# Weight remainders and the rescaling of high words moved to GpSimd in a fused attention, MLP and expert kernel

## The chip, the cores and the metric

The kernel runs on one core of a Trainium2 chip. The metric is the device time of one execution in microseconds; the time before is the median of three runs. TensorE (PE) does matmuls, VectorE (DVE) and ScalarE (ACT) elementwise work, GpSimd (POOL) elementwise work and the issue of indirect DMAs, SyncE (SP) issues the other DMAs. Each engine runs its own queue in order and waits on semaphores for the others.

## The reference

Three layers on 4608 tokens of width 512:

```python
# 1. attention over keys and values that are means of 8 neighbours (576 -> 72), 8 batches, 8 heads of 64
scores = q @ k_pooled.T / 8;  attn = softmax(scores);  x = attn @ v_pooled
# 2. MLP with softplus, 512 -> 2048 -> 512
h = x @ w_in;  g = maximum(h, 0) + log1p(exp(-abs(h)));  x = g @ w_out
# 3. tokens with x @ w_skip > 0 go to the best of 8 experts (512 -> 1024 -> 512), gated
out[do] = xc + gate * (relu(xc @ w1[e]) @ w2[e]);  the other rows of out are x
```

The MLP's weights w_in and w_out reach the kernel as 64-bit floats, read as pairs of 32-bit words ("wbits"); the kernel makes 32-bit floats of them itself.

## The kernel before

**Precision by pairs.** Each matmul operand is kept as a rounded part and a remainder (xh and xl, wh and wl, gh and gl), and a product is three matmuls: high by high, high by low, low by high. The remainder is the value less its rounded part, one subtraction with two inputs in SBUF.

**Stages.** The first layer and the MLP run together, in 9 groups of 512 tokens. `p1(g, c)` computes chunk c (of 16) of the hidden layer for group g (12 matmuls into a bank h, L700), then the softplus: three ScalarE steps (L703 to L705), VectorE's L706 (reads h from PSUM and a from SBUF), ScalarE's rounding L708 and VectorE's remainder L710. `p2` multiplies the result with the output weights (12 matmuls, L721 to L723), two chunks behind p1. The attention for group g + 1 is fed in between as four units of small steps; its softmax shares are multiplied on GpSimd (L536), and its scores are turned with SyncE's "et" transfers (L644). After the groups come the experts, which this change does not touch.

**The weights.** They stay in SBUF for all groups and are unpacked once, during the attention of group 0 and the MLP of group 0, by `load_weights`, a generator that the main loop advances step by step. For each chunk a DMA brings the raw words; `unpack` rescales the high words by a power of two (L467) and turns the low words into small integers (L469), both on ScalarE; `join` puts them together with two VectorE operations (L472, L474), each with two SBUF inputs; ScalarE rounds (L489 or L511); VectorE subtracts (L491 or L512). Chunks 0 to 3 go in halves of 512 columns (L491), chunks 4 to 15 as two halves of 1024 for each pair of chunks' tile: the raw words stand in a tile raw and the result takes the same place as a tile wt. Within one such pair the loop reads:

```python
for j in range(2):
    lo, hi = raw[:, j, :, 0], raw[:, j, :, 1]
    unpack(lo, hi)
    yield
    v = scratch.tile([P, 1024], I32, tag="raw", name="v")
    join(v, lo, hi)
```

**What sets the order.** A scheduler places the instructions of the first two layers on each engine's queue when the kernel is built, by the program's order and its own estimate of when inputs are ready; so a changed engine moves other instructions too. The experts' part is in hand-written order.

Of the kernel before, what the change touches and what calls it, by code (L numbers as in the profile page):

```python
# [9 lines left out]
F32 = mybir.dt.float32  # L10
# [4 lines left out]
AF = mybir.ActivationFunctionType  # L15
ALU = mybir.AluOpType
# [18 lines left out]
def tile_kernel(ctx, tc, qT, kT, vT, wbits, w9, w1, w2, out):  # L35
    nc = tc.nc
# [379 lines left out]
    def wtile(slot, name, *shape, dtype=F32):  # L416
        return wpool.tile([P, *shape], dtype, tag=f"w{slot}", name=name)

    with ExitStack() as ph:
# [41 lines left out]
        def load_weights():  # L461


            bits = wbits.bitcast(I32)

            def unpack(lo, hi):
                nc.scalar.activation(out=hi.bitcast(F32), in_=hi.bitcast(F32), func=AF.Copy,  # L467
                                     scale=2.0 ** -112)
                nc.scalar.activation(out=lo, in_=lo.bitcast(U32), func=AF.Copy, scale=7.49 * 2.0 ** -32)  # L469

            def join(v, lo, hi):
                nc.vector.scalar_tensor_tensor(out=v, in0=hi, scalar=3, in1=lo,  # L472
                                               op0=ALU.logical_shift_left, op1=ALU.bitwise_or)
                nc.vector.scalar_tensor_tensor(out=v, in0=hi, scalar=-0x80000000, in1=v,  # L474
                                               op0=ALU.bitwise_and, op1=ALU.bitwise_or)

            for c in range(EARLY):
                if c % 2 == 0:
                    wt.append(wtile(c // 2, f"wt{c // 2}", 2, 2, 1024, dtype=F32R))
                for j in range(2):  # L480
                    wh, wl = (wt[c // 2][:, c % 2, i, j * 512:(j + 1) * 512] for i in range(2))
                    raw = scratch.tile([P, 512, 2], I32, tag="raw", name="raw")
                    nc.sync.dma_start(out=raw.rearrange("p a b -> p (a b)"),
                                      in_=bits[c * P:(c + 1) * P, j * 1024:(j + 1) * 1024])
                    lo, hi = raw[:, :, 0], raw[:, :, 1]
                    unpack(lo, hi)
                    yield
                    join(lo, lo, hi)
                    nc.scalar.activation(out=wh, in_=lo.bitcast(F32), func=AF.Copy)  # L489
                    yield  # L490
                    nc.vector.tensor_tensor(out=wl, in0=lo.bitcast(F32), in1=wh.bitcast(F32),  # L491
                                            op=ALU.subtract)
                    yield
            for i in range(EARLY // 2, 8):
                raw = wtile(i, f"raw{i}", 2, 1024, 2, dtype=I32)
                for j in range(2):
                    c = 2 * i + j
                    nc.sync.dma_start(out=raw[:, j].rearrange("p a b -> p (a b)"), in_=bits[c * P:(c + 1) * P, :])
                vs = []
                for j in range(2):  # L500
                    lo, hi = raw[:, j, :, 0], raw[:, j, :, 1]
                    unpack(lo, hi)
                    yield
                    v = scratch.tile([P, 1024], I32, tag="raw", name="v")
                    join(v, lo, hi)
                    vs.append(v.bitcast(F32))
                    yield
                wt.append(wtile(i, f"wt{i}", 2, 2, 1024, dtype=F32R))
                for j in range(2):
                    wh, wl = wt[i][:, j, 0], wt[i][:, j, 1]  # L510
                    nc.scalar.activation(out=wh, in_=vs[j], func=AF.Copy)  # L511
                    nc.vector.tensor_tensor(out=wl, in0=vs[j], in1=wh.bitcast(F32), op=ALU.subtract)  # L512
                    yield

        pooled = {}
# [197 lines left out]
        def p2(g, c, gh, gl):  # L713
# [4 lines left out]
            for t in range(T):  # L718
# [4 lines left out]
                nc.tensor.matmul(y, lhsT=tl, rhs=wh, start=False, stop=c == 15)  # L723

        wl = load_weights()
        loaded = [0]

# [262 lines left out]
```

## Time and profile before

| | us |
|---|---|
| median of 3 runs (lowest, highest) | 1374.81 (1373.69, 1377.25) |
| profiled execution | 1388.66 |
| its span | 1386.9 |
| busy in the span: PE, DVE, ACT, POOL | 1338.3, 849.8, 594.7, 307.6 |

The profiled execution is one run with the hardware's recorder on. Its span goes from the first to the last recorded instruction. Busy shares are averages over stages with different limits, so the stretches below matter more than the totals. Matmul ends are modelled, so a busy PE is not PE at its peak.

### The profile page before, as it was taken

How to read it: one execution, taken by the hardware profiler on the slowest of the kernel's cores; microseconds unless marked ns; L12 is line 12 of the kernel's file. 1: busy time of each engine (PE TensorE's matmuls, PEld its weight loads, DVE VectorE, ACT ScalarE, POOL GpSimd, SP SyncE). 2: the span in 40 equal slices, each digit the busy share in tenths (PEclk: the TensorE clock that was granted, in tenths of full speed). 3: DMA queues.
4: the chain of work that ended last, by engine and by line, in shares of the span. 5: the costliest groups of instructions: out<-in, count | busy, mean ns of one | idle time of the engine just before them, and what ended most of it. 6: DMA issues, size and time to landing. Idle time of an engine off the chain costs nothing. (4 is left out here: it accounts for less than half of the span.)

```text
span 1386.9 us, 21423 instructions
## 1 busy us (share of the span) xinstructions
PE 1338.3 (96%) x6970; PEld 1107.7 (80%) x6970; DVE 849.8 (61%) x1955; ACT 594.7 (43%) x1076; POOL 307.6 (22%) x374
## 2 busy tenths in 40 slices
PE   5899999999999999999999999999999999999996
PEld 3567777877878778788778778888989988889885
DVE  7798694784874974965946838534645422325254
ACT  5995554554545555455445445541111111104142
POOL 2000012011021021030020120342424252323233
PEclk9999999999999999999999999999999999999998
DMA  8652243142241241441421301512323122215272
GB/s 285 225 173 75 56 126 95 55 116 63 69 123 43 79 127 28 112 105 31 118 67 39 101 12 52 185 47 84 95 68 108 55 77 62 74 56 173 64 266 81
DMA packets 149599, 134.16 MB, mean 97 GB/s; under 512 B 100789, under 2 KB 116789, under 8 KB 146912
## 3 DMA queue, kind: packets, MB, share of 16 engines
q1 hardware_dynamic: 131744, 95.51, 23.9%
q0 software_dynamic: 17728, 37.13, 8.4%
q8 instruction: 59, 0.97, 0.3%
q14 instruction: 68, 0.56, 0.1%
HBM read 166.67 MB, written 29.67 MB: 142 GB/s over the span
## 5 line engine op out<-in xcount | busy, mean ns | idle before, releaser
L700 PE MATMUL h<-xh,wt 128*128 128x512 f32 x1152 | 383.4, 394 | 3.7 <-DVE a L706 3.4
L700 PEld LDWEIGHTS h<-xh,wt 128*128 128x128 f32 x1152 | 217.4, 189 | 52.4 <-DVE a L706 4.3
L873 PE MATMUL h<-xt,w1h 128*128 128x256 f32 x1280 | 228.1, 281 | 7.5 <-issue 4.5
L721 PE MATMUL y<-wt,gh 128*128 128x512 f32 x576 | 232.9, 404 | 0.0
L118 DVE CUSTOM_DVE_ANT_0 junk<-rows,w9b 128x512 bf16<-128x512 f32 x324 | 222.5, 687 | 8.1 <-ACT rows L112 3.2
L700 PE MATMUL h<-xl,wt 128*128 128x512 f32 x576 | 226.1, 393 | 1.0 <-DVE xl L562 1.0
L722 PE MATMUL y<-wt,gh 128*128 128x512 f32 x576 | 225.3, 391 | 0.0
L723 PE MATMUL y<-wt,gl 128*128 128x512 f32 x576 | 224.9, 391 | 0.0
L873 PEld LDWEIGHTS h<-xt,w1h 128*128 128x128 f32 x1280 | 197.6, 189 | 11.3 <-issue 7.3
L873 PE MATMUL h<-xt,w1l 128*128 128x256 f32 x640 | 180.2, 282 | 3.0 <-issue 1.4
L877 ACT ACTIVATE hs<-h 128x512 fp32r<-128x512 f32 x80 | 47.5, 598 | 311.8 <-PE h L873 157.1
L703 ACT ACTIVATE a<-h 128x512 f32<-128x512 f32 x144 | 85.8, 596 | 202.0 <-PE h L700 143.6
L706 DVE SCALAR_TENSOR_TENSOR a<-h,a 128x512 f32<-128x512 f32 x144 | 98.6, 685 | 107.2 <-ACT a L705 102.9
L708 ACT ACTIVATE gh<-a 128x512 fp32r<-128x512 f32 x144 | 90.9, 632 | 146.5 <-DVE a L706 144.8
L721 PEld LDWEIGHTS y<-wt,gh 128*128 128x128 f32 x576 | 108.2, 188 | 34.2 <-ACT a L703 7.0
L700 PEld LDWEIGHTS h<-xl,wt 128*128 128x128 f32 x576 | 108.9, 189 | 25.2 <-DVE xl L562 1.7
L723 PEld LDWEIGHTS y<-wt,gl 128*128 128x128 f32 x576 | 108.1, 188 | 23.7 <-issue 0.2
L873 PEld LDWEIGHTS h<-xt,w1l 128*128 128x128 f32 x640 | 122.7, 192 | 3.6 <-issue 1.7
L722 PEld LDWEIGHTS y<-wt,gh 128*128 128x128 f32 x576 | 108.3, 188 | 20.6 <-issue 0.8
L710 DVE TENSOR_TENSOR gl<-a,gh 128x512 fp32r<-128x512 f32 x144 | 99.1, 688 | 39.6 <-ACT gh L708 38.2
L897 PE MATMUL y<-w2h,hs 128*128 128x512 f32 x304 | 118.6, 390 | 1.6 <-ACTq L935 1.6
L899 PE MATMUL y<-w2h,hs 128*128 128x512 f32 x304 | 118.6, 390 | 0.8 <-DVE hs L878 0.8
(190 smaller groups left out, 1721.1 us busy)
## 6 DMA issues: line engine op xcount, KB each, us to landing
w9b<-w SPq DMA_DIRECT2D x81, 256.0 KB
raw<-wbits SPq DMA_DIRECT2D x12, 1024.0 KB
x2d<-rows SPq DMA_DIRECT2D x36, 260.0 KB
et<-q SPq DMA_DIRECT2D x256, 32.0 KB
kv<-kT SPq DMA_DIRECT2D x28, 288.0 KB
kv<-vT SPq DMA_DIRECT2D x28, 288.0 KB
xm<-misc SPq DMA_DIRECT2D x160, 32.0 KB
misc<-misc SPq DMA_DIRECT2D x144, 32.0 KB
```

The costliest lines, as they stand in the source:

```text
L118: nc.vector.tensor_tensor_reduce(out=ws["junk"], in0=rows[t][:, :D], in1=w9b[e], scale=1.0, scalar=0.0, op0=ALU.mult, op1=ALU.add, accum_o ...
L700: nc.tensor.matmul(h, lhsT=l, rhs=r[:, kk, :], start=n == 0, stop=n == 11)
L703: nc.scalar.activation(out=a, in_=h, func=AF.Abs)
L706: nc.vector.scalar_tensor_tensor(out=a, in0=h, scalar=0.0, in1=a, op0=ALU.max, op1=ALU.add)
L708: nc.scalar.activation(out=gh, in_=a, func=AF.Copy)
L710: nc.vector.tensor_tensor(out=gl, in0=a, in1=gh.bitcast(F32), op=ALU.subtract)
L721: nc.tensor.matmul(y, lhsT=th, rhs=wh, start=c == 0, stop=False)
L722: nc.tensor.matmul(y, lhsT=th, rhs=wl, start=False, stop=False)
L723: nc.tensor.matmul(y, lhsT=tl, rhs=wh, start=False, stop=c == 15)
L873: nc.tensor.matmul(h[:, f2, :], lhsT=l, rhs=r[:, kk, :], start=n == 0, stop=n == 11)
L897: nc.tensor.matmul(y, lhsT=hh[:, f, js], rhs=ws["w2h"][:, f, :], start=f == 0, stop=False)
L899: nc.tensor.matmul(y, lhsT=hl[:, f, js], rhs=ws["w2h"][:, f, :], start=False, stop=f == 7)
```

## The change

GpSimd takes over every weight subtraction (L491, L512; L495 and L516 after), and for chunks 4 to 15 the rescaling of the high words (L467; L468 after). The low words, the joins and the rounding stay where they were, as does the rescaling for chunks 0 to 3. Lines below the helper move down by four.

```diff
-            def unpack(lo, hi):
-                nc.scalar.activation(out=hi.bitcast(F32), in_=hi.bitcast(F32), func=AF.Copy,
-                                     scale=2.0 ** -112)
+            def unpack(lo, hi, pool=False):
+                if pool:
+                    nc.gpsimd.tensor_scalar(out=hi.bitcast(F32), in0=hi.bitcast(F32), scalar1=2.0 ** -112,
+                                            scalar2=None, op0=ALU.mult)
+                else:
+                    nc.scalar.activation(out=hi.bitcast(F32), in_=hi.bitcast(F32), func=AF.Copy,
+                                         scale=2.0 ** -112)
                 nc.scalar.activation(out=lo, in_=lo.bitcast(U32), func=AF.Copy, scale=7.49 * 2.0 ** -32)
...
-                    nc.vector.tensor_tensor(out=wl, in0=lo.bitcast(F32), in1=wh.bitcast(F32),
+                    nc.gpsimd.tensor_tensor(out=wl, in0=lo.bitcast(F32), in1=wh.bitcast(F32),
                                             op=ALU.subtract)
...
-                    unpack(lo, hi)
+                    unpack(lo, hi, True)
...
-                    nc.vector.tensor_tensor(out=wl, in0=vs[j], in1=wh.bitcast(F32), op=ALU.subtract)
+                    nc.gpsimd.tensor_tensor(out=wl, in0=vs[j], in1=wh.bitcast(F32), op=ALU.subtract)
```

In the order lists below the number in a name is that of its buffer. For chunks 4 to 15 the pairs are raw_496 and wt_547, raw_552 and wt_624, raw_629 and wt_724, raw_748 and wt_842, raw_885 and wt_977, raw_1003 and wt_1098.

VectorE, while the tile for chunks 6 and 7 is joined, before:

```order
L472 SCALAR_TENSOR_TENSOR v<-raw_552 128x1024
L512 TENSOR_TENSOR wt_547<-v,wt_547 128x1024 x2
L706 SCALAR_TENSOR_TENSOR a<-h,a 128x512
L474 SCALAR_TENSOR_TENSOR v<-raw_552,v 128x1024
L710 TENSOR_TENSOR gl<-a,gh 128x512
L472 SCALAR_TENSOR_TENSOR v<-raw_552 128x1024
L472 SCALAR_TENSOR_TENSOR v<-raw_629 128x1024
L474 SCALAR_TENSOR_TENSOR v<-raw_552,v 128x1024
L474 SCALAR_TENSOR_TENSOR v<-raw_629,v 128x1024
L706 SCALAR_TENSOR_TENSOR a<-h,a 128x512
L512 TENSOR_TENSOR wt_624<-v,wt_624 128x1024
```

The same place after (L476 and L478 are the joins, L710 and L714 the softplus steps, L642 and L524 attention):

```order
L476 SCALAR_TENSOR_TENSOR v<-raw_552 128x1024
L642 STREAM_TRANSPOSE q<-q 128x768
L478 SCALAR_TENSOR_TENSOR v<-raw_552,v 128x1024
L476 SCALAR_TENSOR_TENSOR v<-raw_552 128x1024
L710 SCALAR_TENSOR_TENSOR a<-h,a 128x512
L478 SCALAR_TENSOR_TENSOR v<-raw_552,v 128x1024
L714 TENSOR_TENSOR gl<-a,gh 128x512
L476 SCALAR_TENSOR_TENSOR v<-raw_629 128x1024
L524 TENSOR_REDUCE kp<-kv 128x72
L478 SCALAR_TENSOR_TENSOR v<-raw_629,v 128x1024
```

The subtractions have left, and joins, softplus steps and attention follow each other directly.

GpSimd, from the softmax shares of group 0 (written to boot_kv) to those of the first two attention units of group 1 (q), before:

```order
L536 TENSOR_TENSOR boot_kv<-boot_kv,boot_171 128x576 x4
L633 MEMSET q 128x8x24
L536 TENSOR_TENSOR q<-q,st 128x8x72
L633 MEMSET q 128x8x24
L536 TENSOR_TENSOR q<-q,st 128x8x72
```

The queue after, around the same two multiplications on q (L540 now):

```order
L468 TENSOR_SCALAR raw_629<-raw_629 128x1024
L540 TENSOR_TENSOR q<-q,st 128x8x72
L516 TENSOR_TENSOR wt_547<-v,wt_547 128x1024 x2
L468 TENSOR_SCALAR raw_629<-raw_629 128x1024
L468 TENSOR_SCALAR raw_748<-raw_748 128x1024
L516 TENSOR_TENSOR wt_624<-v,wt_624 128x1024 x2
L637 MEMSET q 128x8x24
L516 TENSOR_TENSOR wt_724<-v,wt_724 128x1024 x2
L540 TENSOR_TENSOR q<-q,st 128x8x72
L468 TENSOR_SCALAR raw_748<-raw_748 128x1024
L468 TENSOR_SCALAR raw_885<-raw_885 128x1024
L516 TENSOR_TENSOR wt_842<-v,wt_842 128x1024 x2
```

Between two multiplications of shares there now stand rescales, each of which waits for its raw tile's DMA, and pairs of subtractions.

SyncE's DMA issues, around the last raw tile, before; the "et" rows that follow are those of the second attention unit of group 1:

```order
L498 DMA raw_885<-wbits 128x2048
L498 DMA raw_1003<-wbits 128x2048
L609 DMA kv<-kT 128x576
L498 DMA raw_1003<-wbits 128x2048
L644 DMA et<-q 32x8x32 x2
```

After, the second half of raw_1003 stands behind the "et" rows of the third unit, of which the last ones are shown:

```order
L648 DMA et<-q 32x8x32 x2
L648 DMA et<-q 8x8x32
L502 DMA raw_1003<-wbits 128x2048
L526 DMA kv<-vT 128x576
L648 DMA et<-q 32x8x32 x2
```

The raw words' transfer has moved behind two more series of twelve "et" transfers.

## Rows read from the trace of the kernel before

**Rows 1.** The page: span and busy time of each engine.

```profile
span 1386.9 us, 21423 instructions
...
PE 1338.3 (96%) x6970; PEld 1107.7 (80%) x6970; DVE 849.8 (61%) x1955; ACT 594.7 (43%) x1076; POOL 307.6 (22%) x374
```

**Rows 2.** Busy time by stretch: start:end, length, then as its heading says.

```profile
core 0: us, PE busy (x) PEld busy (x) DVE busy (x) ACT busy (x) POOL busy (x), PEclk, DMA share, GB/s
10.00:45.00 35.00, 25.19 (x87) 14.46 (x87) 27.21 (x52) 26.37 (x51) 5.37 (x4) 1.00 0.81 294
128.00:820.00 692.00, 690.26 (x3223) 548.60 (x3223) 482.63 (x1241) 347.36 (x675) 107.94 (x142) 1.00 0.30 80
45.00:128.00 83.00, 77.08 (x347) 58.09 (x346) 79.20 (x105) 70.60 (x112) 5.27 (x8) 0.98 0.44 147
50.00:60.00 10.00, 9.51 (x35) 7.65 (x36) 9.55 (x16) 9.69 (x15) 1.51 (x1) 0.83 0.94 371
60.00:120.00 60.00, 56.05 (x254) 42.36 (x254) 58.72 (x72) 50.59 (x81) 3.16 (x4) 1.00 0.38 118
```

**Rows 3.** Who waited for whom on PE, 44 to 80 us: total, times, longest.

```profile
PE h L700 <- DVE a L706: 3.4, 2, 2.0
```

**Rows 4.** VectorE groups by form, 45 to 128 us: busy us, mean ns.

```profile
L472 DVE SCALAR_TENSOR_TENSOR v<-raw 128x1024 int32<-128x1024 int32 x12 | 15.6, 1318 | 0.0
L512 DVE TENSOR_TENSOR wt<-v,wt 128x1024 fp32r<-128x1024 f32 x12 | 15.1, 1272 | 0.2 <-ACT wt L511 0.2
L474 DVE SCALAR_TENSOR_TENSOR v<-raw,v 128x1024 int32<-128x1024 int32 x12 | 14.4, 1210 | 0.0
L710 DVE TENSOR_TENSOR gl<-a,gh 128x512 fp32r<-128x512 f32 x12 | 8.2, 683 | 0.9 <-ACT gh L708 0.7
...
L491 DVE TENSOR_TENSOR wt<-raw,wt 128x512 fp32r<-128x512 f32 x3 | 2.1, 685 | 0.0
```

**Rows 5.** VectorE timeline, pairs: start, us for both.

```profile
70.29 2.35 DVE L474 SCALAR_TENSOR_TENSOR v<-raw,v 128x1024 int32<-128x1024 int32 x2
...
43.89 1.29 DVE L562 SCALAR_TENSOR_TENSOR xl<-o,xh 128x512 fp32r<-128x512 f32 x2 [2.94 <-ACT xh L561]
```

**Rows 6.** ScalarE groups by form, 45 to 128 us.

```profile
L467 ACT ACTIVATE raw<-raw 128x1024 f32<-128x1024 f32 x10 | 11.6, 1160 | 0.0
```

**Rows 7.** Timeline of GpSimd (POOL) and VectorE at three meetings.

```profile
56.32 1.51 POOL L536 TENSOR_TENSOR q<-q,st 128x576 f32<-128x576 f32 x1 [7.48 <-ACT wt L489]
...
56.73 0.68 DVE L706 SCALAR_TENSOR_TENSOR a<-h,a 128x512 f32<-128x512 f32 x1
57.33 1.58 DVE L472 SCALAR_TENSOR_TENSOR v<-raw 128x1024 int32<-128x1024 int32 x1
...
84.77 1.15 POOL L536 TENSOR_TENSOR q<-q,st 128x576 f32<-128x576 f32 x1 [5.41 <-ACT wt L511]
...
85.12 1.89 DVE L512 TENSOR_TENSOR wt<-v,wt 128x1024 fp32r<-128x1024 f32 x1
...
105.42 1.49 POOL L536 TENSOR_TENSOR q<-q,st 128x576 f32<-128x576 f32 x1 [5.54 <-DVE st L535]
...
105.82 2.17 DVE L472 SCALAR_TENSOR_TENSOR v<-raw 128x1024 int32<-128x1024 int32 x1
```

**Rows 8.** GpSimd groups by form, whole span.

```profile
L752 POOL MEMSET xg<- 128x1040 f32 x1 | 1.0, 975 | 9.5 <-PE h L700 9.5
...
masks.py:199 POOL TENSOR_SCALAR_AFFINE_SELECT ident<-ident 128x128 f32<-128x128 f32 x1 | 0.3, 284 | 0.0
...
masks.py:197 POOL MEMSET ident<- 128x128 f32 x1 | 0.2, 205 | 0.3 <-POOLq L981 0.3
```

**Rows 9.** Timeline at the last two weight tiles: VectorE, TensorE, SyncE's DMA queue.

```profile
126.58 1.22 DVE L512 TENSOR_TENSOR wt<-v,wt 128x1024 fp32r<-128x1024 f32 x1
...
132.28 0.39 PE L700 MATMUL h<-xh,wt 128*128 128x512 f32 x1
...
137.72 0.39 PE L700 MATMUL h<-xh,wt 128*128 128x512 f32 x1
...
108.95 8.20 SPq L644 DMA_DIRECT2D et<-q  x12
```

## The prediction

> **What bounds the kernel now.** I read the page's busy times first, then the busy times by stretch, then the waits of TensorE, then the VectorE groups of one stretch, and last the timeline. The page has TensorE at 1338.3 us of 1386.9 [rows 1]; by stretch, it works 690.26 of the 692 us from 128 to 820 [rows 2]. So anything that makes the first 128 us longer or shorter goes to the end undiminished, and nothing can be won later. In the stretch from 45 to 128 us, where chunks 4 to 15 are unpacked, TensorE has 77.08 of 83 us, so its waits are 5.9 us; VectorE has 79.20 and ScalarE 70.60 [rows 2]. From 60 to 120 VectorE is idle for only 1.3 us of 60 [rows 2]. Of TensorE's waits, 3.4 us are for VectorE's softplus step L706 [rows 3]. In this stage VectorE is the second bound, a few per cent behind TensorE, and the change unloads it. GpSimd looks free, with 5.27 us of 83 [rows 2]. Whether it is free is the question.
>
> The profiled execution took 1388.66 us (span 1386.9), 13.85 us more than the median of the three runs shown, 1374.81. I work out a difference on the profiled execution and carry it to the median unchanged, since it arises in one stage. About 0.3%, 4.1 us, is what a measurement of this kernel can tell from no change.
>
> **What leaves VectorE and ScalarE.** Neighbouring VectorE instructions overlap a little, so the price of one is the step from one start to the next: a pair of 1024-column operations takes 2.35 us and one alone 1.21, so 1.14 each; a pair of 512-column ones 1.29 against 0.68, so 0.61 [rows 4, 5]. In the stage, twelve L512 subtractions and three L491 leave [rows 4]: 12 x 1.14 + 3 x 0.61 = 15.5 us. Ten of the twelve high-word rescales (L467) fall in the stage, at 1.16 us [rows 6]; ScalarE loses about 11 us. ScalarE is not what TensorE's waits name, so I credit that nothing by itself.
>
> **What GpSimd takes on.** The trace has no subtraction and no scalar multiply on GpSimd. Its two-input operation L536 takes 1.15 us for 576 columns when nothing is in its way [rows 7]. Memsets give a fixed part: 0.975 us for 1040 columns, 0.205 for 128, so 0.84 ns a column and 0.10 us fixed [rows 8]. Then L536 costs (1.15 - 0.10)/576 = 1.83 ns a column, a subtraction of 1024 columns 1.97 us, of 512 columns 1.03. For the rescale, with one input, the bound below is the memset's rate, 0.96 us. The one operation with one input and one output, the affine select, gives (0.284 - 0.10)/128 = 1.46 ns a column [rows 8], 1.59 us. The bound above is the two-input price, 1.97. I take 1.28, midway between the memset and the affine select, and keep 0.96 and 1.97 for the range. In the stage that makes 12 x 1.97 + 3 x 1.03 + 10 x 1.28 = 39.5 us of new GpSimd work.
>
> **What the new work does to VectorE.** L536 met a VectorE operation with two SBUF operands three times in this stage, and each time VectorE stood still [rows 7]. L512 issued at 85.12 took 1.89 us, with L536 running from 84.77 to 85.92. L472 took 1.58 at 57.33 and 2.17 at 105.82, each with L536 beside it. The same form never met takes 1.21 (L474) [rows 4]. The excess is 0.37 + 0.68 + 0.96 = 2.01 us, for three L536 of 1.15 us. The wait goes both ways: two of these L536 took 1.51 and 1.49. L706, with one operand in PSUM, kept its 0.68 in the middle of it [rows 7]. So the two engines exclude each other whenever VectorE reads two SBUF operands, and 2.01 of 3.45 us, 58%, of GpSimd's time was lost to VectorE.
>
> What VectorE keeps is mostly of the excluded kind: both join operations (24 x 1.14 = 27.4 us, and four of 512 columns, 2.4) and L710 (12 x 0.61 = 7.3), 37.1 us together. With GpSimd's 39.5 + 3.45 that is 80.1 us of mutually exclusive work in a stage of 83. Before, it was 37.1 + 15.5 + 3.45 = 56 us. There is no way left to hide it well.
>
> The sum: 58% of 39.5 is 22.9 us blocked, against 15.5 saved, so VectorE has 7.4 us more to do. Its idle time of 60 to 120, 1.3 us, can take that much. Ahead of the stage, from 10 to 45 us, five subtractions leave (3.1 us) and 5 x 1.03 + 2 x 1.28 = 7.7 us arrive, at 58% 4.5: another +1.4, of which I count half, because VectorE is idle there for 7.8 of 35 us [rows 2] but the first x tiles hang on its order. 7.4 - 1.3 + 0.7 = **6.8 us slower**: 1395.5 in a profiled execution like this one, **1381.6** against the median. For bounds, the share blocked in the single meetings is 0.37/1.15 = 32% and 0.96/1.15 = 83%: 39.5 us at these gives VectorE -2.9 and +17.3 us. The rescale at 0.96 gives 36.3 us of work and +5.6 at 58%; at 1.97, 46.4 us and +11.4.
>
> The Trainium skill, "GPSIMD Engine Reference", section "Performance versus the Vector engine", speaks against the change: it measures a two-input operation on GpSimd at 4497 ns for 2048 columns, about twice VectorE's time, and its section "Performance pitfalls for Q7 kernels" gives about 1.9 cycles a column for reads at steps up to 8 bytes, which is the step of the high words. By its figures, as an estimate, a subtraction would be 2.25 us and a rescale 1.62, the new work 46.6 us, and the sum +11.5 instead of +7.4 for VectorE. No run here has shown either yet.
>
> **What waits behind what.** GpSimd's queue is in order: L468 for a raw tile waits for that tile's DMA, and behind it stand L540 (the softmax shares) and the L516 pairs. Its stage total, 39.5 + 5.3 of 83 us, leaves room. SyncE's queue changes more: the second half of raw_1003 was issued ahead of the second attention unit's "et" transfers, and now stands behind the third unit's, which end at 108.95 + 8.20 = 117.2 us [rows 9]. After it lands there are a rescale (1.28), the low words and the rounding on ScalarE (at most 1.16 each), two joins (2.3) and a subtraction (1.97): 7.9 us. Chunk 15's matmuls start at 137.72 [rows 9], so 12.6 us remain for a transfer of 1 MB, about 3.6 us at the 294 GB/s of 10 to 45 us [rows 2]. I cost it at nothing; it would begin to cost if that issue were 9 us late against TensorE.
>
> **The rivals.**
> *Faster.* If less than 15.5/39.5 = 39% of GpSimd's new time blocks VectorE, VectorE gains. That happens if the rescale, with only one input, doesn't exclude VectorE, or if holds fall beside port-free work (VectorE keeps some 24 us of it). At 32% VectorE is 2.9 us better, ScalarE 11 us, and TensorE gets back up to its 5.9 us of waits: 1369. For it: one meeting of three was at 32%. Against it: a longer hold outlasts the port-free operations (mostly 0.6 to 0.75 us) more, and the 80 us of exclusive work leave no room.
> *No change.* The last weight remainder is done at 127.7 and first needed after 132.28 [rows 9]: 4.5 us of lead, plus VectorE's idle time outside 60 to 120. If the lateness is mostly in weights and not in L706 and L710, this swallows it: about +2, 1377. Against it: L706 and L710 stand in the same queue as the blocked joins.
> *Heavier.* With the rescale at the two-input price VectorE has +11.4, so 1386; at 83% blocked it has 38.5 - 15.5 = +23.0, so 1397. TensorE's longer waits could cost more by its clock, which in 50 to 60 us, after a wait of about 2 us on L706 [rows 3], was granted 0.83 on the mean, so partly the lower of its two levels [rows 2]. I put this case at 1390.
>
> **How the numbers follow.** The forecast (1379 to 1386) has 0.44, heavier 0.20, no change 0.22, faster 0.14. Slower by over 0.3% is 0.64. The range, 1371 to 1394, leaves out about half of the faster case and the last third of the heavier one. The forecast's own range is 1379 to 1386.
>
> **What would show it.** In the profile after: the subtraction on GpSimd near 1.97 us and the rescale near 1.28 where unhindered; the joins and L714 above 1.21 and 0.68 whenever GpSimd runs; VectorE as full as before in 60 to 120 although twelve operations left; ScalarE clearly emptier; TensorE's waits on L710 (the softplus step's new line) longer; and 128 us onwards unchanged but shifted. I am wrong if the joins keep their 1.21 us beside a rescale, or if the stage ends earlier than before.

## The result and the profile after

| | before | after |
|---|---|---|
| median of 4 runs each (lowest, highest), us | 1375.10 (1373.69, 1377.25) | 1393.79 (1390.77, 1396.03) |
| ratio, 95% interval | | 1.0133 (1.0110, 1.0157) |
| profiled execution, us | 1388.66 | 1390.77 |

The change costs 18.7 us, 1.33%, where 6.8 us were forecast. The two profiled executions lie only 2.1 us apart, because that of before was 13.6 us above its median; so the comparison below goes by stages. Where that surplus lies is seen from the first softplus step of the MLP's very last chunk, before and after:

```profile
912.91 0.60 ACT L703 ACTIVATE a<-h 128x512 f32<-128x512 f32 x1 [0.82 <-DVE gl L710]
...
928.91 0.60 ACT L707 ACTIVATE a<-h 128x512 f32<-128x512 f32 x1 [0.82 <-DVE gl L714]
```

From there to the end of the span it is 1386.9 - 912.91 = 474.0 us before and 1389.1 - 928.91 = 460.2 after. Nearly all of that time belongs to the experts' part, which the change doesn't touch. (The profiles of e4 to e7 further down have 471 to 477 us there, those of the other versions 460 to 463.) TensorE works 619.47 of the 620 us from 200 to 820 after the change, so in the MLP's later groups nothing is lost or won.

How late the stage is can be read from one event: the softplus of the last chunk, c = 15 of group 0, starts with ScalarE's first step (L703 before, L707 after). ScalarE's timeline (start, us) has it before at

```profile
142.93 0.60 ACT L703 ACTIVATE a<-h 128x512 f32<-128x512 f32 x1 [0.82 <-DVE gl L710]
```

and after at the last row of this piece; the first two rows belong to a place that is read further down.

```profile
60.93 0.62 ACT L709 ACTIVATE a<-a 128x512 f32<-128x512 f32 x1
...
69.12 0.63 ACT L712 ACTIVATE gh<-a 128x512 fp32r<-128x512 f32 x1 [6.54 <-DVE a L710]
...
159.85 0.60 ACT L707 ACTIVATE a<-h 128x512 f32<-128x512 f32 x1 [2.67 <-PE h L704]
```

It is 16.9 us late in these two executions, nearly the whole 18.7, and at the MLP's last chunk it is still 16.0. So the stretch up to 143 us before stands against that up to 160 us after. Before, by stretch:

```profile
core 0: us, PE busy (x) PEld busy (x) DVE busy (x) ACT busy (x) POOL busy (x), PEclk, DMA share, GB/s
0.00:143.00 143.00, 121.14 (x514) 88.13 (x515) 117.41 (x178) 106.79 (x181) 15.10 (x54) 0.99 0.55 186
45.00:143.00 98.00, 92.08 (x416) 70.12 (x415) 86.73 (x117) 77.88 (x126) 6.67 (x9) 0.98 0.44 143
```

After, the same columns:

```profile
45.00:128.00 83.00, 65.71 (x269) 48.70 (x268) 65.45 (x77) 49.68 (x83) 58.57 (x26) 0.90 0.38 131
60.00:120.00 60.00, 45.60 (x185) 33.01 (x184) 43.91 (x51) 32.29 (x54) 41.86 (x19) 0.89 0.33 106
200.00:820.00 620.00, 619.47 (x2901) 493.19 (x2900) 438.88 (x1139) 311.63 (x606) 98.61 (x132) 1.00 0.30 81
45.00:160.00 115.00, 94.72 (x394) 70.41 (x393) 85.75 (x100) 65.77 (x110) 73.15 (x33) 0.91 0.39 129
0.00:160.00 160.00, 125.56 (x510) 89.88 (x511) 117.49 (x160) 96.16 (x170) 94.53 (x86) 0.94 0.50 170
```

TensorE's idle time up to chunk 15 goes from 143 - 121.14 = 21.9 us to 160 - 125.56 = 34.4, which is +12.6; its busy time rises by 4.4 us for nearly as many matmuls (514 and 510), at a granted clock of 0.94 of full speed on the mean instead of 0.99. Together that is 17.0 us. VectorE's busy time is nearly the same, 86.73 and 85.75 us, but in a stretch 17 us longer: in 60 to 120 us it works 43.91 us, where [rows 2] have 58.72. GpSimd rises from 6.67 to 73.15 us.

Who waited for whom in 45 to 160 us after (total, times, longest), TensorE and VectorE:

```profile
PE h L704 <- DVE a L710: 17.3, 4, 7.5
...
DVE q L642 <- POOL q L540: 6.3, 4, 2.8
```

TensorE's wait for the softplus step, 3.4 us in [rows 3], is now 17.3. VectorE waits for GpSimd 11.6 us, 6.3 for the shares and 5.3 for late subtractions and rescales (the row of L476 below); from 45 to 143 us before it was 0.8. The groups by form that answer to [rows 4] and [rows 6], 45 to 160 us after (busy us, mean ns, idle time before):

```profile
L516 POOL TENSOR_TENSOR wt<-v,wt 128x1024 fp32r<-128x1024 f32 x12 | 32.2, 2705 | 13.6 <-ACT wt L515 13.6
L468 POOL TENSOR_SCALAR raw<-raw 128x1024 f32<-128x1024 f32 x10 | 32.1, 3222 | 4.4 <-DMA raw<-wbits 4.4
...
L476 DVE SCALAR_TENSOR_TENSOR v<-raw 128x1024 int32<-128x1024 int32 x11 | 21.5, 1957 | 5.3 <-POOL wt L516 3.1 <-POOL raw L468 2.2
L478 DVE SCALAR_TENSOR_TENSOR v<-raw,v 128x1024 int32<-128x1024 int32 x12 | 17.6, 1470 | 0.0
L714 DVE TENSOR_TENSOR gl<-a,gh 128x512 fp32r<-128x512 f32 x15 | 14.9, 992 | 5.7 <-ACT gh L712 5.7
```

A rescale holds GpSimd 3.22 us and a subtraction 2.70. The joins and L714 became longer by 11 x 0.64 + 12 x 0.26 + 15 x 0.31 = 14.8 us against [rows 4]; three joins of 512 columns add 1.5 us (1.13, 1.13 and 1.28 us each, 0.68 before). These 16.3 us are about what left VectorE (15.5).

How this reaches TensorE is seen at its longest wait. GpSimd and VectorE, timeline:

```profile
57.36 3.34 POOL L468 TENSOR_SCALAR raw<-raw 128x1024 f32<-128x1024 f32 x1
60.66 1.16 POOL L540 TENSOR_TENSOR q<-q,st 128x576 f32<-128x576 f32 x1
61.77 5.64 POOL L516 TENSOR_TENSOR wt<-v,wt 128x1024 fp32r<-128x1024 f32 x2
67.37 7.68 POOL L468 TENSOR_SCALAR raw<-raw 128x1024 f32<-128x1024 f32 x2
...
61.85 0.98 DVE L642 STREAM_TRANSPOSE q<-q 128x768 f32<-128x768 f32 x1 [1.86 <-POOL q L540]
62.75 2.45 DVE L478 SCALAR_TENSOR_TENSOR v<-raw,v 128x1024 int32<-128x1024 int32 x1
65.13 3.35 DVE L476 SCALAR_TENSOR_TENSOR v<-raw 128x1024 int32<-128x1024 int32 x1
68.41 0.68 DVE L710 SCALAR_TENSOR_TENSOR a<-h,a 128x512 f32<-128x512 f32 x1
69.01 1.51 DVE L478 SCALAR_TENSOR_TENSOR v<-raw,v 128x1024 int32<-128x1024 int32 x1
...
71.05 1.21 DVE L476 SCALAR_TENSOR_TENSOR v<-raw 128x1024 int32<-128x1024 int32 x1
```

ScalarE's L709 had the input of L710 ready at 61.55 (above), but L710 starts at 68.41. Ahead of it in VectorE's queue stand the transpose L642, which waits for the shares L540, which stand in GpSimd's queue behind a rescale of 3.34 us; and two joins that take 2.45 and 3.35 us under two subtractions. The rescales from 67.37 on hardly slow the joins beside them (1.51 and 1.21 us). TensorE then resumes after its longest wait:

```profile
69.14 0.80 PE L704 MATMUL h<-xh,wt 128*128 128x512 f32 x1 [7.54 <-DVE a L710]
```

Its matmul here takes 0.80 us, where 0.39 is usual.

### The profile page after: what moved, and what is told of

The parts are those of the page before. It is cut to its first block, busy times and chain, and to the rows that moved or that the text cites. A ratio compares the mean times of both kernels' runs of the same rounds, so it can differ in the third digit from the quotient of the medians.

```text
span 1389.1 us, 21437 instructions
## 1 busy us (share of the span) xinstructions
PE 1337.7 (96%) x6970; PEld 1109.0 (80%) x6970; DVE 849.1 (61%) x1935; ACT 584.1 (42%) x1064; POOL 388.5 (28%) x406
## 5 line engine op out<-in xcount | busy, mean ns | idle before, releaser
L704 PE MATMUL h<-xh,wt 128*128 128x512 f32 x1152 | 386.0, 396 | 17.6 <-DVE a L710 17.3
L707 ACT ACTIVATE a<-h 128x512 f32<-128x512 f32 x144 | 85.9, 596 | 207.0 <-PE h L704 150.8
L710 DVE SCALAR_TENSOR_TENSOR a<-h,a 128x512 f32<-128x512 f32 x144 | 98.6, 685 | 106.3 <-ACT a L709 105.7
L714 DVE TENSOR_TENSOR gl<-a,gh 128x512 fp32r<-128x512 f32 x144 | 103.8, 721 | 44.0 <-ACT gh L712 43.9
L903 PE MATMUL y<-w2h,hs 128*128 128x512 f32 x304 | 118.4, 390 | 1.3 <-DVE hs L882 1.3
L905 DVE SCALAR_TENSOR_TENSOR ys<-y,xg 128x512 f32<-128x512 f32 x38 | 28.5, 751 | 147.2 <-PE y L903 147.2
```

What stands on the lines that cost most here:

```text
L704: nc.tensor.matmul(h, lhsT=l, rhs=r[:, kk, :], start=n == 0, stop=n == 11)
L707: nc.scalar.activation(out=a, in_=h, func=AF.Abs)
L710: nc.vector.scalar_tensor_tensor(out=a, in0=h, scalar=0.0, in1=a, op0=ALU.max, op1=ALU.add)
L714: nc.vector.tensor_tensor(out=gl, in0=a, in1=gh.bitcast(F32), op=ALU.subtract)
L903: nc.tensor.matmul(y, lhsT=hl[:, f, js], rhs=ws["w2h"][:, f, :], start=False, stop=f == 7)
```

## The experiments

Two theories stood against each other. **A, the queue:** GpSimd's instructions are so long that its in-order queue is late, and VectorE's in-order queue waits for it, with L710 behind the waiting instruction. **B, the exclusion:** a GpSimd subtraction and a VectorE operation with two SBUF operands stop each other. All ratios are to the kernel before, run beside it on the same chip, with a 95% interval. The runs e4 to e7 were on a chip on which the kernel before itself took 1387.64 us, so their times compare only by ratio.

| run | what differs | us | ratio |
|---|---|---|---|
| e1 | after, rescale back on ScalarE | 1383.20 | 1.0066 (1.0046, 1.0087) |
| e2 | after, all subtractions back on VectorE | 1378.46 | 1.0026 (1.0015, 1.0037) |
| e3 | before, early subtractions alone on GpSimd | 1376.04 | 1.0013 (1.0001, 1.0024) |
| e4 | after, group 1's shares on VectorE | 1406.13 | 1.0129 (1.0102, 1.0156) |
| e5 | before, group 1's shares on VectorE | 1387.40 | 0.9993 (0.9981, 1.0006) |
| e6 | e1, one input in place of the late subtraction | 1388.85 | 1.0009 (0.9996, 1.0023) |
| e7 | before, rescale of two pairs' tiles on GpSimd | 1389.62 | 1.0018 (1.0004, 1.0032) |
| e8 | after, one input in place of the late subtraction | 1384.35 | 1.0077 (1.0058, 1.0095) |
| e9 | after, softplus result kept in PSUM | 1393.77 | 1.0130 (1.0113, 1.0146) |
| e10 | before, softplus result kept in PSUM | 1373.73 | 0.9993 (0.9984, 1.0002) |
| e11 | after, half of each rescale on ScalarE | 1381.66 | 1.0052 (1.0035, 1.0069) |
| e12 | e11, GpSimd's queue padded again | 1395.07 | 1.0155 (1.0138, 1.0172) |
| e13 | e1, GpSimd's queue padded | 1405.56 | 1.0234 (1.0217, 1.0251) |

### The prices by themselves (m1_prices)

A small kernel that leaves the whole computation out, and runs three of each GpSimd operation alone, then beside joins.

```diff
+    for i in (3, 4, 5):
+        scale(i)           # GpSimd: the rescale, on every second word
+    for i in (0, 1, 2, 0, 1, 2):
+        join(i)            # VectorE, on other tiles
...
+    for i in (0, 1, 2):
+        minus(i)           # GpSimd: the subtraction
+    for i in (3, 4, 5, 3, 4, 5):
+        join(i)
```

> Leaves out the whole computation: it only measures, on one core, the moved operations on 128 x 1024 columns, three of each in a row, first alone and then beside VectorE joins (step 1.14 us each). Theory A (the price of the rescale): the rescale in place on every second word takes 2.8 to 3.2 us on GpSimd even alone, about twice or more what the same multiply takes on adjacent words (1.0 to 1.6 us), and the joins beside it lose little, at most 0.4 us each. Theory B (exclusion): alone the rescale takes under 2 us, its 3.2 us in the changed kernel are waits for VectorE, and beside it the joins stand still for the whole of it. Both expect the subtraction alone at 1.97 to 2.35 us and the joins stopped for the whole of it.

Timeline of GpSimd, then of VectorE (start, us for all of a row):

```profile
10.16 8.48 POOL L64 TENSOR_SCALAR raw<-raw 128x1024 f32<-128x1024 f32 x3
...
19.19 8.23 POOL L67 TENSOR_SCALAR fa<-fa 128x1024 f32<-128x1024 f32 x3
...
27.97 6.93 POOL L70 TENSOR_TENSOR fl<-fa,fh 128x1024 fp32r<-128x1024 f32 x3
...
48.77 10.15 POOL L64 TENSOR_SCALAR raw<-raw 128x1024 f32<-128x1024 f32 x3
...
71.09 9.88 POOL L70 TENSOR_TENSOR fl<-fa,fh 128x1024 fp32r<-128x1024 f32 x3
...
44.06 3.49 DVE L74 SCALAR_TENSOR_TENSOR vj<-raw 128x1024 int32<-128x1024 int32 x3
...
47.54 8.66 DVE L74 SCALAR_TENSOR_TENSOR vj<-raw 128x1024 int32<-128x1024 int32 x6
...
69.86 13.33 DVE L74 SCALAR_TENSOR_TENSOR vj<-raw 128x1024 int32<-128x1024 int32 x6
```

Alone, a rescale takes 8.48/3 = 2.83 us, nearly the same on adjacent words (L67, 2.74), so the step of the words isn't what makes it long, as theory A had it; a subtraction takes 2.31, a join 1.16. Six joins beside three rescales take 1.44 us each: the two overlap, at a loss of 0.28 a join and 0.56 a rescale. Six joins beside three subtractions take 13.33 us, close to the sum of the two alone (6.93 + 6 x 1.16 = 13.9): these do exclude each other.

### The change in parts (e1, e2, e3)

e1 undoes the rescale's move, e2 that of both subtractions, and e3 makes the move of the eight 512-column subtractions alone.

```diff
-                    unpack(lo, hi, True)
+                    unpack(lo, hi)
```

```diff
-                    nc.gpsimd.tensor_tensor(out=wl, in0=vs[j], in1=wh.bitcast(F32), op=ALU.subtract)
+                    nc.vector.tensor_tensor(out=wl, in0=vs[j], in1=wh.bitcast(F32), op=ALU.subtract)
```

> The subtractions on GpSimd, the rescale back on ScalarE. Theory A: most of the loss goes with the rescale; GpSimd has some 30 us of work in the stage instead of 58, so 1375 to 1382. Theory B: the subtractions are what excludes the joins, so the loss stays, 1386 to 1394.

> The rescale of chunks 4 to 15 on GpSimd, the subtractions back on VectorE. Theory A: 12 x 3 us in front of the joins in an in-order queue; VectorE is as full as before and its joins come later: 1380 to 1390. Theory B: without the subtractions' holds nearly nothing is left of the loss, 1372 to 1378.

> Only the eight half-chunk subtractions of chunks 0 to 3 on GpSimd, all else as before. Both theories: within 0.3% of the kernel before, 1371 to 1379, since VectorE has idle time in the first 45 us; a third theory, that the first x tiles come later because shares wait behind subtractions in GpSimd's queue, expects 1380 or more.

The subtractions alone cost 0.66%, between the two expectations; the rescale alone 0.26%, just outside both; the early subtractions 0.13%. No part explains 1.33% by itself, and 0.66 and 0.26 together make 0.92. The remaining 0.41 points appear only when both are moved.

### The shares (e4, e5)

If what hurts is that the shares L540 stand behind rescales, VectorE can multiply them for group 1.

```diff
-            return [(unit if g else unit0)(hp, [(b * 4 + hp, *r) for b, *r in part], xh, xl) for hp in range(4)]
+            us = [[(b * 4 + hp, *r) for b, *r in part] for hp in range(4)]
+            if g == 1:
+                return [unit(hp, us[hp], xh, xl, nc.vector) for hp in range(4)]
+            return [(unit if g else unit0)(hp, us[hp], xh, xl) for hp in range(4)]
```

> The changed kernel, with the softmax shares of group 1 (four multiplications, 1.15 us each on GpSimd) back on VectorE. Theory A, as it stands after the first runs: VectorE stands idle in its queue for results that wait behind rescales and subtractions in GpSimd's queue; with the shares out of that queue the transposes no longer wait for it (6.3 us in the changed kernel), less about 2.4 us of new VectorE work: 1386 to 1391. Theory B (exclusion alone): work only moves, 1391 to 1396.

> Control: the kernel before with the same four multiplications on VectorE. Both theories: VectorE waited 0.8 us for them before and now has about 2.4 us more work in a stage where it is nearly full: 1373 to 1378.

e4 stays at 1.29%, as theory B had it. VectorE no longer waits for shares, but still for rescales and subtractions, in 45 to 170 us:

```profile
DVE v L476 <- POOL wt L516: 4.5, 2, 3.1
DVE v L476 <- POOL raw L468: 2.8, 1, 2.8
```

That is 7.3 us, where the changed kernel had 5.3, and the four multiplications take VectorE 3.9 us, where 2.4 were expected. So taking this one wait away wins nothing. That the wait was harmless isn't shown by it, since the scheduler also placed other instructions in another order. On the kernel before, the same edit changes nothing that can be measured (e5).

### The exclusion alone (e6, e8)

GpSimd multiplies the rounded part by 2^-12, one input, in place of the late subtraction. The remainders of chunks 4 to 15 are then not computed; GpSimd's queue keeps its number of instructions, and every queue its order up to 160 us. One thing more changes: GpSimd no longer reads the joined tile v, so a buffer of v (there are three) comes free a step earlier.

```diff
-                    nc.gpsimd.tensor_tensor(out=wl, in0=vs[j], in1=wh.bitcast(F32), op=ALU.subtract)
+                    nc.gpsimd.tensor_scalar(out=wl, in0=wh.bitcast(F32), scalar1=2.0 ** -12, scalar2=None,
+                                            op0=ALU.mult)
```

> As the run with only the subtractions on GpSimd, but for chunks 4 to 15 GpSimd multiplies the rounded part by a constant (one input) where it subtracted (two inputs): so the remainders of these chunks are not computed. The multiply takes 2.8 us alone, the subtraction 2.3. Theory B: nothing excludes the joins any more, 1373 to 1379. Theory A (GpSimd's durations and its in-order queue): at least as slow as with the subtraction, 1382 to 1388.

> The changed kernel, rescale on GpSimd included, but GpSimd multiplies the rounded part of chunks 4 to 15 by a constant (one input) where it subtracted; the remainders of these chunks are not computed. GpSimd has more to do than in the changed kernel (2.8 us for 2.3, twelve times), in the same queue. Theory B (exclusion makes the loss, the part that rescale and subtraction have only together included): 0 to 0.4% above the kernel before, about what the rescale alone costs. Theory A (queue and durations): 0.8% or more above it.

From e1 to e6 the ratio falls from 1.0066 to 1.0009, and from the change to e8 from 1.0133 to 1.0077: 0.57 and 0.56 points, 7.8 us, twice the same. e6 came out as theory B had it, e8 between the two theories. The groups of e8, 45 to 160 us, with the wait of TensorE and that of VectorE for the shares:

```profile
L516 POOL TENSOR_SCALAR wt<-wt 128x1024 fp32r<-128x1024 f32 x12 | 35.0, 2919 | 8.1 <-ACT wt L515 7.3
...
L476 DVE SCALAR_TENSOR_TENSOR v<-raw 128x1024 int32<-128x1024 int32 x11 | 15.9, 1449 | 3.0 <-POOL raw L468 3.0
L478 DVE SCALAR_TENSOR_TENSOR v<-raw,v 128x1024 int32<-128x1024 int32 x12 | 15.1, 1261 | 0.0
...
PE h L705 <- DVE a L711: 13.3, 3, 6.1
...
DVE q L643 <- POOL q L541: 9.8, 4, 4.7
```

The joins fell from 1957 and 1470 ns to 1449 and 1261. Yet 0.77 points stay, with VectorE waiting 9.8 + 3.0 = 12.8 us for GpSimd and TensorE 13.3 for VectorE. Exclusion is a cause, and by far not the only one. The multiply holds GpSimd a little longer than the subtraction did (2919 ns against 2705), so by that 0.56 points is rather too little for the exclusion than too much. The earlier release of v works the other way: the changed kernel waited once for it, 3.1 us (L476 for L516), and e8 doesn't. But e1 had no such wait, and there the edit is worth the same.

The same two runs show that the price of a full queue isn't the sum of its parts. The twelve multiplies with no rescale beside them leave e6 at 0.09%, with GpSimd busy for 45.1 us of the 115; the rescales alone cost 0.26 (e2); both together, 75.4 us of 115, cost 0.77 (e8).

### Fewer rescales (e7)

Rescale on GpSimd only for two of the six pairs' tiles (`unpack(lo, hi, i < 4)` in the kernel before).

> The kernel before with the rescale on GpSimd for the first two raw tiles only (chunks 4 to 7). Theory A: little waits for them there, since GpSimd's queue is nearly empty before 65 us, and ScalarE loses 4.6 us of the stretch in which it is fullest: 1371 to 1377. Theory B: the same, a rescale excludes nothing.

At 1.0018 it cannot be told from e2's 1.0026, whose interval it overlaps; it decides nothing.

### Which VectorE operation carries the loss (e9, e10)

The softplus result is written over its bank h in PSUM, so that L714 has one SBUF operand only.

```diff
-            nc.vector.scalar_tensor_tensor(out=a, in0=h, scalar=0.0, in1=a, op0=ALU.max, op1=ALU.add)
+            nc.vector.scalar_tensor_tensor(out=h, in0=h, scalar=0.0, in1=a, op0=ALU.max, op1=ALU.add)
...
-            nc.scalar.activation(out=gh, in_=a, func=AF.Copy)
+            nc.scalar.activation(out=gh, in_=h, func=AF.Copy)
...
-            nc.vector.tensor_tensor(out=gl, in0=a, in1=gh.bitcast(F32), op=ALU.subtract)
+            nc.vector.tensor_tensor(out=gl, in0=h, in1=gh.bitcast(F32), op=ALU.subtract)
```

> The changed kernel, with the softplus result kept in its PSUM bank, so that the softplus remainder (L714) has one SBUF operand only and is not excluded; the joins still are. If the loss reaches TensorE through L714 standing still (0.3 us each on the mean), the distance to the kernel before falls from 1.33% to 0.9% or less. If it comes through the joins in front of the softplus steps, it stays at 1.1 to 1.4%.

> Control and candidate: the kernel before with the softplus result kept in its PSUM bank. The tile a is free one step earlier, the bank h one step later. Both theories: within 0.3% of the kernel before; a gain of some us if ScalarE's waits for the remainder (4.4 us up to 128 us) reached TensorE, a loss if the two banks are now held too long.

In e9 L714 does fall from 992 to its undisturbed time:

```profile
L714 DVE TENSOR_TENSOR gl<-h,gh 128x512 fp32r<-128x512 f32 x15 | 10.2, 679 | 2.8 <-ACT gh L712 2.8
```

That saves 4.7 us of VectorE's work, and the time stays at 1.0130. So freeing L714 from the exclusion wins nothing. How much of the loss L714 carried in the changed kernel stays open, for the bank h is now held until L714 has read it, and TensorE waits for that, 45 to 160 us:

```profile
PE h L704 <- DVE gl L714: 5.2, 2, 3.4
```

The scheduler also placed other instructions in another order here. On the kernel before, the edit gives 0.9993, no measurable gain.

### The queue alone (e11, e12, e13)

e11 leaves GpSimd 512 columns of each rescale and gives ScalarE the others:

```diff
-                    nc.gpsimd.tensor_scalar(out=hi.bitcast(F32), in0=hi.bitcast(F32), scalar1=2.0 ** -112,
-                                            scalar2=None, op0=ALU.mult)
+                    nc.gpsimd.tensor_scalar(out=hi[:, :512].bitcast(F32), in0=hi[:, :512].bitcast(F32),
+                                            scalar1=2.0 ** -112, scalar2=None, op0=ALU.mult)
+                    nc.scalar.activation(out=hi[:, 512:].bitcast(F32), in_=hi[:, 512:].bitcast(F32),
+                                         func=AF.Copy, scale=2.0 ** -112)
```

e12 adds two operations of 256 columns on GpSimd behind each, whose result nobody needs, on a tile of their own; their one tie to the rest is a column of the raw tile that they read as a scalar. e13 adds four such operations in each place of e1 where the change has a rescale.

```diff
+    pad = const.tile([P, 256], F32, name="pad")
+    nc.gpsimd.memset(pad, 1.0)
...
+                    for _ in range(2):
+                        nc.gpsimd.tensor_scalar(out=pad, in0=pad, scalar1=hi[:, 0:1].bitcast(F32), scalar2=None, op0=ALU.max)
```

> The changed kernel, with each rescale of chunks 4 to 15 halved: GpSimd does the first 512 columns, ScalarE the other 512 (0.66 us each). By the runs so far the changed kernel's 1.33% is 0.56% exclusion by the subtractions and 0.77% that needs the rescale, the early halves and GpSimd's full queue. If the second part comes from the time that the rescale holds GpSimd's queue, halving it (17 us less on GpSimd) takes off more than the rescale costs alone when halved (0.13%): 0.8 to 1.1% above the kernel before remain. If the order of the queue and not its fill makes it, 1.2 to 1.4% remain.

> The kernel with the halved rescale (0.52% above the kernel before), with two GpSimd operations of 256 columns on a tile of their own behind each halved rescale, about 1.5 us together; the joins don't wait for them. If the fill of GpSimd's queue is what costs, the loss comes back: 1.0 to 1.4% above the kernel before. If it is the way from the rescale to its join, or the order, it stays at 0.4 to 0.8%.

> The kernel with only the subtractions on GpSimd (0.66% above the kernel before), with four GpSimd operations of 256 columns on a tile of their own for each rescale that ScalarE does, about 3 us together; nothing but GpSimd's later work waits for them. If the fill of the queue costs, 1.0 to 1.4% above the kernel before; if the loss needs joins that wait for a rescale on GpSimd, 0.5 to 0.8%.

Taking half of the rescales off GpSimd gives back 0.81 of the 1.33 points, more than was expected (0.52% remain, where 0.8 to 1.1 were named). Padding takes 1.03 away again, also more than was expected (1.55%, not 1.0 to 1.4), but its two operations take 2.7 us and not 1.5. From 45 to 160 us GpSimd is busy for 63.1 us in e11, 73.2 in the changed kernel and 86.4 in e12, the order of their times. e13 loses 1.68 points over e1, but can't be counted: the rounding overwrites the raw tile and must wait until the padding has read its column, and ScalarE's waits in 45 to 160 us show that this became a wait of its own, in e13

```profile
ACT wt L519 <- POOL pad L510: 19.1, 4, 5.6
```

and in e12 once, for 2.1 us:

```profile
ACT wt L521 <- POOL pad L473: 2.1, 1, 2.1
```

The joins and VectorE's waits for GpSimd, 45 to 160 us, in e11:

```profile
L480 DVE SCALAR_TENSOR_TENSOR v<-raw,v 128x1024 int32<-128x1024 int32 x12 | 20.6, 1716 | 0.0
...
L716 DVE TENSOR_TENSOR gl<-a,gh 128x512 fp32r<-128x512 f32 x17 | 18.0, 1060 | 4.1 <-ACT gh L714 4.0
L478 DVE SCALAR_TENSOR_TENSOR v<-raw 128x1024 int32<-128x1024 int32 x11 | 17.4, 1578 | 1.8 <-POOL raw L468 0.8 <-issue 0.6 <-ACT raw L475 0.4
...
DVE q L644 <- POOL q L542: 2.4, 2, 1.3
```

and in e12:

```profile
L482 DVE SCALAR_TENSOR_TENSOR v<-raw 128x1024 int32<-128x1024 int32 x12 | 19.3, 1611 | 9.3 <-POOL wt L522 3.6 <-POOL raw L470 3.4 <-POOL wt L501 1.8
L484 DVE SCALAR_TENSOR_TENSOR v<-raw,v 128x1024 int32<-128x1024 int32 x12 | 17.2, 1434 | 0.0
L720 DVE TENSOR_TENSOR gl<-a,gh 128x512 fp32r<-128x512 f32 x14 | 16.3, 1166 | 2.2 <-ACT gh L718 2.2
...
DVE q L648 <- POOL q L546: 8.6, 3, 5.3
```

The joins of e12 are not longer than those of e11: 24 take 36.5 us, 1.52 each, against 23 in 38.0, 1.65 each. What is longer is VectorE's waiting for GpSimd: 2.4 + 0.8 = 3.2 us in e11, 8.6 + 3.6 + 3.4 + 1.8 = 17.4 in e12. That is 14.2 us more, and 1.03 points are 14.2 us; that the two are equal is chance, since a wait of VectorE need not reach TensorE, and two other things are longer by 3.5 us together: the softplus remainder (L720, 1.17 us for 1.06) and a small step of the softmax (L544, 0.66 us for 0.16, four times). No join reads the padding's tile, its one tie was waited for once, 2.1 us, and the queues kept e11's order but for two copies at the very start. So here the fill of the queue makes most of the loss.

## Why the prediction was right in its direction and wrong in its size

**Held: the bound and the direction.** The stage up to chunk 15 lost 16.9 us and the MLP's later groups gained nothing; TensorE's wait on the softplus step rose from 3.4 to 17.3 us; ScalarE is emptier (65.77 us from 45 to 160, 77.88 from 45 to 143 before) and that brought no gain. (One slip: the last remainder before is done at 126.58 + 1.22 = 127.8, not 127.7, which changes nothing.)

**Failed: the price of the rescale.** The step took 1.28 us, midway between a memset and an affine select, with the two-input price as the bound above. The runs have 2.83 alone and 3.22 in the stage: the one-input multiply is longer than the two-input subtraction, so the bound above was wrong too. The subtraction, forecast at 1.97, took 2.31 alone and 2.70 in the stage. In place of 39.5 us GpSimd got 32.2 + 32.1 + 3.5 = 67.8 us, in 45 to 160. With the prices that m1 measured (and 1.03 kept for 512 columns), the step's own sum would have been 12 x 2.31 + 3 x 1.03 + 10 x 2.83 = 59.1 us, 58% of that 34.3, and 34.3 - 15.5 - 1.3 + 0.7 = 18.2 us. That is the measured size, but by luck: the blocked share was far smaller, and waits made up for it. The estimates from the Trainium skill, "GPSIMD Engine Reference", sections "Performance versus the Vector engine" (2.25 us for a subtraction) and "Performance pitfalls for Q7 kernels" (1.62 for a rescale), stand against the same runs: the first is near 2.31, the second far under 2.83, and the measurement decides.

**Failed, and this is the larger part: the in-order queue of GpSimd costed at nothing.** The prediction read the stage total, 45 of 83 us, as room. With the real prices it is 73 of 115, and what stands in that queue is waited for by VectorE, whose own queue holds the softplus step L710 behind the wait. Of the 1.33 points, 0.77 (10.6 us) stay when the late subtraction no longer excludes VectorE (e8), of which the early subtractions alone would make 0.13 (e3); e11, with less in the queue, has 0.52 left with the exclusion still in it; and e12 brings the loss back with waits and no longer joins.

**Half right: the exclusion.** For subtractions it is real and complete (m1), and those of chunks 4 to 15 are worth 0.56 points, 7.8 us (e6, e8). But the step applied it to the rescale as well, at 58% of the hold. A rescale costs a join 0.28 us; the sign of being wrong that the prediction named, joins that keep 1.21 us beside a rescale, came out at 1.21 to 1.51 in the timeline and 1.44 in m1. In all, VectorE lost 16.3 of 67.8 us, 24%, below the lower bound of 32%. The faster rival's condition was less than 15.5 us blocked; VectorE came out about even, and its busy time did not grow (85.75 us, 86.73 before). The kernel became slower all the same, since VectorE now stands waiting for GpSimd for 11.6 us. "VectorE as full as before" is refuted.

**Held: SyncE's late issue of raw_1003 at nothing.** From 120 to 160 us TensorE waited 3.0 us on attention (vr, L547) and for no weight, though GpSimd once waited 4.4 us for a raw tile's transfer.

**The rival that came nearest** is the heavier one, 1386 to 1397. Its clause on the clock held: granted 0.90 in 45 to 128 instead of 0.98, and 4.4 us more for nearly as many matmuls, behind waits of up to 7.5 us. Its own mechanism, more blocking of VectorE by the rescale, did not.

**Open.** In e11 the scheduler also placed some instructions in another order, on GpSimd and the other engines, and how much of its 0.81 points that gave was not tried; e12 kept e11's order, so the loss that fill makes doesn't hang on it. The changed kernel's own order differs from that of before as well, and no run has it without the moved work, so a part of the 0.77 points may be the order's. The exclusion and the queue were not shown to add up: they act on the same waits, and 0.56 and 0.77 are only the split in which the exclusion is taken away first. No version here beats the kernel before beyond the interval (e5 and e10, 0.9993 each).

## What to carry to other kernels

An engine that is idle for 94% of a stage is free only as far as nothing that stands in line elsewhere waits for its queue: ask for each moved instruction what it stands ahead of on the new engine, and what stands behind the one that waits for it. An operation's price doesn't move with it, and the number of inputs doesn't bound it: measure it alone on the engine it moves to, and beside the neighbour that it will meet, which here took one small kernel. Read an engine's busy time together with its waits, since VectorE's busy time was unchanged here while TensorE's wait for it grew fivefold.

## What the runs showed of the hardware that was not expected

- On GpSimd, a multiply by a constant of 128 x 1024 32-bit floats takes 2.74 us on adjacent words and 2.83 on every second word, longer than a subtraction of two inputs of that size, 2.31. Why was not found.
- A subtraction on GpSimd and a VectorE operation with two SBUF inputs run one after the other (13.33 us for work of 6.93 and 6.9); a multiply by a constant overlaps with it, and slows it from 1.16 to 1.44 us (m1). It isn't the one input alone that does it: a copy of 8 columns, with one input too, took GpSimd 0.19 us alone and 1.11 beside a join (m1).
- GpSimd's small operations are dear too: 256 columns of a one-input operation, its constant read from a tile, took 1.36 us each in e12, where a rescale of 512 columns took 1.94.
